# Layer 2: x1 to the output at once, the expert output copied by ScalarE and added there by GpSimd's transfers, for 13 of 16 tiles

## The chip, the core and the metric

The kernel runs on one core of a Trainium2 chip. The core has TensorE (PE in the profile), VectorE (DVE), ScalarE (ACT), GpSimd (POOL) and SyncE (SP), each with its own queue of instructions that it works through in order; they wait for each other through semaphores. Transfers between device memory and the on-chip memory are started by an instruction on an engine's queue and then run on 16 DMA engines beside the five engines. Until now SyncE starts every transfer here. The metric is the time of one execution on the device in microseconds (us).

## The reference: what is computed

The input x has 2048 rows of 576 values. Two layers of two blocks run one after the other with the same weights:

```python
x = A_x
x = x + _A_ref(_layernorm(x), A_wqkv, A_wo)               # linear attention
x = x + _B_ref(_layernorm(x), B_w_q, B_k1, B_k2, B_u, B_v)  # expert layer
x = x + _A_ref(_layernorm(x), A_wqkv, A_wo)
x = x + _B_ref(_layernorm(x), B_w_q, B_k1, B_k2, B_u, B_v)
```

`_A_ref` makes q, k and v (32 heads of 18), passes q and k through phi (t + 1 above 0, exp(t) otherwise), sums k times v over all rows into one state, and gives q times that state over a denominator, times `A_wo`. `_B_ref` scores each row against two small key tables per head, takes the best expert of each head, weighs the chosen rows of `B_v` with gelu of the products with `B_u`, and sums them. The last line's sum is the output: x1, the stream after the second attention, plus the expert output.

## The kernel before

The rows are cut into 16 tiles of 128 rows (t from 0 to 15), so a tile of the stream is 128x576 in float32. A product in float32 is split into a high and a low part on ScalarE and VectorE (`split`, L117 and L118: `hi` by ScalarE's copy, `lo` by VectorE's subtraction) and done in several passes on TensorE. Names in the profile carry a prefix: `thio`/`tloo` are the split attention output of a tile, `thib`/`tlob` the split normalised input of the expert layer (with the expert counts of an earlier tile as a sixth block), `pto`/`ptb` their transposes, `ppo` the product with `A_wo`, `pps` the scores, `ppq` the late q product, `po` the expert output.

In layer 2 a tile passes through these steps, each a generator that stops at its `yield`s, so that the steps of several tiles can be woven together:

- `num` (`back_scale`, L453 to L463): GpSimd makes o from q and the state's sums, VectorE reduces the denominator `den` and divides, GpSimd copies a strip.
- `oT` (`back_oT`): transpose on TensorE, split, a small cast on GpSimd (L468).
- `O` (`back_out`, L483): 28 matrix products into `ppo`; then `residual` (L473), one VectorE instruction that adds x and sums each row, writing x1 (`x11_t`); then the layer norm of x1: GpSimd makes the negative mean `mb` (L187), ScalarE squares and sums (L188, output `junk`), GpSimd makes scale and shift `rsb` (L193 to L195), ScalarE writes the normalised `yb` (L205).
- `bc` (`exp_T`): transposes of `yb` and of the counts `cg` into `ptb`, split.
- `S` (`exp_scores`, L525): 14 products into `pps`, and ScalarE's copy to `s` (L530).
- `sel` (`exp_select`, L553 to L590): thirteen small VectorE instructions that find the experts, ending in `cg`; `gel` (`exp_gelu`, L539 to L545): gelu between ScalarE and GpSimd, in one buffer `g`.
- `po` (`exp_out`, L609): four products into `po`, then the end of the tile. For tiles 0 to 9 and 13 to 15 this is `residual` again: VectorE adds `po` and x1 into x2 (`x21_t`), and SyncE stores it to `out` (L623). For tiles 10, 11 and 12 TensorE has put x1 into `po` beforehand (`base`, L598), and ScalarE copies the finished sum to x2 (L613), which SyncE stores.

The order in which the steps stand on TensorE, ScalarE, VectorE and GpSimd is written out by hand: `play` takes a text such as `O1.4 bc1.3,2x2 sel1.13`, runs one piece of a step for each word (step, layer, tile), and `in_order` holds these four engines to that order. SyncE keeps the order in which its transfers are written. x1 has 6 buffers, x2 has 2, the loaded x has 3, and TensorE's outputs (PSUM) share 4 buffers in turn.

Of the kernel before, what the change touches and what calls it, by code (L numbers as in the profile page):

```python
# [62 lines left out]

@with_exitstack
def network(ctx, tc, x_in, wqkv, wo, wq_t, k_t, u_t, v2, c_mask, c_mask4, c_ident, c_code, c_code1, c_scale, c_shift, out):
    nc = tc.nc
# [117 lines left out]
    def spread(xt, total, n):  # L184

        m = wk.tile([P, 2], F32, tag="mv", name=f"m{n}")
        nc.gpsimd.tensor_scalar(m[:, 0:1], total, -1.0 / D, 1.0, op0=ALU.mult, op1=ALU.mult)  # L187
        nc.scalar.activation(junk, xt, AF.Square, bias=m[:, 0:1], accum_out=m[:, 1:2])  # L188
        return m

    def layernorm_sum(xt, m, n):
        rs = wk.tile([P, 2], F32, tag="rs", name=f"rs{n}")
        nc.gpsimd.tensor_scalar(rs[:, 0:1], m[:, 1:2], 1.0 / D, EPS_LN, op0=ALU.mult, op1=ALU.add)  # L193
# [1 line left out]
        nc.gpsimd.tensor_tensor(rs[:, 1:2], m[:, 0:1], rs[:, 0:1], op=ALU.mult)  # L195
        return normalized(xt, rs, n)

    def normalized(xt, rs, n, vector=False):

        y = wk.tile([P, 2, 320], F32, tag="y", name=f"y{n}", bufs=3)  # L200
        x2 = bass.AP(tensor=xt.tensor, offset=xt.offset, ap=[xt.ap[0], [256, 2], [1, 320]])
        if vector:
            nc.vector.tensor_scalar(y, x2, rs[:, 0:1], rs[:, 1:2], op0=ALU.mult, op1=ALU.add)
        else:
            nc.scalar.activation(y, x2, AF.Identity, scale=rs[:, 0:1], bias=rs[:, 1:2])  # L205
# [270 lines left out]
    def back_out(l, t):  # L476
        n = f"{l}_{t}"
        hl = tt.pop(("oT", l, t))
        p = psum("ppo" + n)
        todo = sorted(out_passes(), key=lambda x: x[1]) if t == 0 else out_passes()  # L480
        for i, (a, b, w, r) in enumerate(todo):
            for c0, c1, at in PARTS:
                nc.tensor.matmul(p[:, at:at + c1 - c0], hl[a][:r, b], w[:r, c0:c1], start=(i == 0), stop=(i == len(todo) - 1))  # L483
# [116 lines left out]
    def exp_out(l, t):  # L600
        n = f"{l}_{t}"
        c = tt.pop(("c", l, t))
        p = tt.pop(("base", l, t), None)
        based = p is not None
        if not based:
            p = psum("po" + n)
        for i in range(2):
            for c0, c1, at in PARTS:
                nc.tensor.matmul(p[:, at:at + c1 - c0], c[i], vmix[:, c0:c1], start=(i == 0 and not based), stop=(i == 1))  # L609
        yield  # L610
        if based:
            x2 = wk.tile([P, D], F32, tag="x2", name=f"x2{n}", bufs=BUFS["x2"])
            nc.scalar.activation(x2, row(p), AF.Copy)  # L613
        else:
            x2, total = residual(p, xs.pop(("b", l, t)), n, "x2")
        if l == 0:
            nc.sync.dma_start(x_d[t], x2)
# [4 lines left out]
        else:
            nc.sync.dma_start(out[t * P:(t + 1) * P, :], x2)  # L623
# [251 lines left out]
    with in_order(*ALL):  # L875

        play("""
            bT0.13 gel0.12 po0.11 sel0.12 v1.10 po0.11x2 gel0.12 num0.15 sel0.12 k1.10 bT0.13 v1.10 sel0.12 fT1.11
            sel0.12 oT0.14 v1.10 fT1.11 O0.14 num0.15 cT0.12 num0.15 k1.10 cT0.12 O0.14 oT0.15 bT0.13 po0.12 S0.13
            O0.14 fT1.11 S0.13 oT0.15 po0.12x3 sel0.13x2 v1.11 gel0.13 fT1.12 gel0.13 oT0.15 O0.14 sel0.13x2 k1.11  # L880
            v1.11 O0.15 fT1.12 O0.15 bT0.14 st1.10 cT0.13 v1.11 bT0.14 S0.14 cT0.13 O0.15 fT1.12 keep1.12 po0.13 k1.11
            S0.14 gel0.14 sel0.14 po0.13 gel0.14 st1.11 po0.13 k1.12 sel0.14x2 po0.13 fT1.13 k1.12 O0.15 v1.12x2
            sel0.14 v1.12 bT0.15 cT0.14x2 st1.12 fT1.13 bT0.15 po0.14 S0.15 po0.14 fT1.13 S0.15 po0.14 ldx1.1 po0.14
            ldx1.3 v1.13 fT1.14 v1.13 sel0.15x3 gel0.15 k1.13 fT1.14 gel0.15 bT0.-1 v1.13 sel0.15 cT0.15 v1.14 cT0.15
            po0.15 k1.13 q1.13 bT0.-1 po0.15 q1.13 v1.14 po0.15x2 v1.14 k1.14 wl1.0 st1.13 fT1.15x2 k1.14 k1.15 v1.15
            rl1.0 st1.14 k1.15 ldq1.13 v1.15x2 rl1.2 st1.15 lq1.0 mk1.0 zs1.0 M1.1 rl1.1 lq1.0 M1.1 rl1.3 ldx1.0 zs1.0
            M1.4x2 M1.3 lq1.1 M1.0 num1.13 num1.0 num1.13 num1.0x2 M1.3 keep1.11 lq1.1 num1.1 M1.0 oT1.0x2 num1.1
            M1.2x2 rl1.4 num1.1 num1.13 lq1.2 O1.0 oT1.1 oT1.13 q1.14 lq1.2 O1.0 oT1.1 O1.0x2 num1.2 q1.14 lq1.3x2
            num1.2 oT1.13 bc1.0,-9 num1.3 O1.1 bc1.0,-9 num1.2 S1.0 O1.1 oT1.2 S1.0 num1.3 lq1.4 gel1.0 num1.3 oT1.2
            O1.1x2 O1.2 bc1.1,-9 sel1.0 gel1.0 ldx1.2 sel1.0 lq1.4 O1.13 rl1.6 bc1.1,-9 sel1.0 num1.4x2 S1.1 O1.2x2  # L890
            ldx1.13 O1.13 S1.1 lq1.6 O1.2 sel1.0 sel1.1 bc1.2,0 rl1.5 ldx1.5 rl1.7 num1.4 oT1.3 ldq1.14 lq1.5 lq1.6
            gel1.1 bc1.2,0 oT1.4 gel1.1 sel1.1 O1.13 rl1.8 sel1.1 S1.2 po1.0 oT1.3 lq1.5 sel1.1 S1.2 O1.3 po1.0 sel1.2
            rl1.9 O1.13 oT1.4 num1.6 bc1.13,1 num1.5 sel1.2 num1.5 lq1.7 bc1.13,1 gel1.2x2 num1.5 S1.13 O1.3 lq1.7
            O1.3x2 num1.6 rl1.11 sel1.2 po1.1 oT1.5 q1.15 oT1.5 ldx1.4 sel1.2 bc1.3,2 po1.1 S1.13 gel1.13 num1.6 O1.4
            bc1.3,2 sel1.13 q1.15 ldx1.6 po1.2 O1.5 oT1.6 ldq1.15 po1.2 sel1.13 num1.14 S1.3 O1.4 lq1.8 O1.4 num1.14
            num1.7 rl1.10 sel1.13 gel1.13 O1.5 num1.14 O1.4 num1.7 S1.3 sel1.13 ldx1.7 sel1.3 oT1.6 num1.7 bc1.4,13
            ldx1.14 bc1.4,13 rl1.12 O1.6 ldx1.8 lq1.8 po1.13 O1.5 gel1.3 O1.5 sel1.3 oT1.7 po1.13 sel1.3 num1.8 O1.6
            S1.4 gel1.3 num1.8 oT1.7 S1.4 sel1.3 sel1.4 gel1.4 sel1.4 oT1.14 bc1.5,3 lq1.9 O1.6 sel1.4 bc1.5,3 S1.5
            po1.3 ldx1.15 O1.6 num1.8 ldx1.11 gel1.4 oT1.8 oT1.14 num1.15 S1.5 sel1.4 bc1.6,4 po1.3 sel1.5 gel1.5
            lq1.9 bc1.6,4 num1.15 O1.14 num1.9 oT1.8 S1.6 O1.14x2 sel1.5 O1.14 S1.6 gel1.5 po1.4 num1.15 sel1.5x2 O1.7  # L900
            po1.4 num1.9 gel1.6 bc1.14,5 O1.7 bc1.14,5 oT1.15 gel1.6 O1.7 sel1.6 num1.9 O1.8 po1.5 S1.14x2 O1.7 po1.5
            oT1.9 sel1.6 O1.8 sel1.6 ldx1.9 O1.8 sel1.6 sel1.14 gel1.14 oT1.15 sel1.14 lq1.10 oT1.9 lq1.10 bc1.7,6x2
            O1.9 gel1.14 O1.8 sel1.14 po1.6 ldx1.10 po1.6 num1.10 S1.7x2 sel1.14 num1.10 O1.9 sel1.7 bc1.8,14 num1.10
            lq1.11 bc1.8,14 po1.14 sel1.7 O1.9 lq1.11 O1.9 gel1.7x2 sel1.7 S1.8 sel1.7 O1.15 S1.8 ldx1.12 gel1.8
            sel1.8 num1.11 po1.14 O1.15 oT1.10 bc1.9,7 gel1.8 sel1.8 bc1.9,7 lq1.12 O1.15 S1.9 sel1.8 oT1.10 num1.11
            sel1.8 lq1.12 O1.15 num1.12 po1.7 S1.9 num1.11 bc1.15,8 gel1.9 po1.7 sel1.9 O1.10 gel1.9 oT1.11 num1.12
            bc1.15,8 O1.10x2 po1.8x2 sel1.9 oT1.11 S1.15x2 sel1.9 O1.11 O1.10 gel1.15 sel1.9 gel1.15 sel1.15 bc1.10,9
            num1.12 O1.11 sel1.15 bc1.10,9 O1.11 oT1.12 S1.10 sel1.15 po1.9 O1.11 sel1.15 oT1.12 S1.10 gel1.10
            bc1.11,15 sel1.10 O1.12 po1.9 gel1.10 bc1.11,15 O1.12x2 S1.11 sel1.10x2 po1.15 sel1.10 po1.15 S1.11
            sel1.11 O1.12 sel1.11 base1.10 bc1.12,10x2 gel1.11x2 sel1.11 S1.12x2 sel1.11 base1.11 gel1.12 sel1.12  # L910
            gel1.12 po1.10 bc1.-1,11x2 base1.12 sel1.12x2 po1.10 sel1.12 po1.11x2 bc1.-1,12x2 po1.12x2
        """)


# [42 lines left out]
```

## Time and profile before

| | |
|---|---|
| time, median of 3 runs | 718.7 us (717.38 to 720.29) |
| the profiled execution's own time | 718.14 us |
| its span, first to last instruction | 716.4 us |
| TensorE busy | 699.6 us, 98% |
| VectorE busy | 475.1 us, 66% |
| ScalarE busy | 321.6 us, 45% |
| GpSimd busy | 201.6 us, 28% |
| mean granted TensorE clock | 0.996 |

The profile is of one execution. A row of its timeline has the start in us from the span's start, the duration in us, the engine, the line, the operation, out<-in with the shapes, how many instructions the row merges, and in brackets how long the engine sat idle before it and whose instruction ended that. Buffer numbers are left out of names, so which tile a row belongs to is found by laying the rows beside the program's own order, which has them. TensorE's instructions are pipelined and their ends are modelled, so that rows of PE overlap a little. The second layer's expert part stands between about 540 us and the end; the first `po` of layer 2 is at 566.7 us.

### The profile page before, as it was taken

The numbers are of one execution on the slowest core, as the hardware profiler recorded it, in microseconds if no ns is written. First come the engines' busy times: TensorE is split into PE (matmuls) and PEld (weight loads), VectorE is DVE, ScalarE is ACT, GpSimd is POOL, SyncE is SP. The second block draws the span as 40 slices with busy tenths as digits, with TensorE's granted clock in tenths as the row PEclk, the third lists the DMA queues.
The fourth block names the chain that finished last, engine by engine and source line by source line (L and its number), as shares of the span: only waits on it lengthen the run. The fifth ranks groups of instructions, "written<-read, shape, count | busy, mean of one in ns | idle before, by whom it ended". The sixth has DMA issues, their size and how long they took to land.

```text
span 716.4 us, 14695 instructions
## 1 busy us (share of the span) xinstructions
PE 699.6 (98%) x5464; PEld 650.7 (91%) x5464; DVE 475.1 (66%) x1031; ACT 321.6 (45%) x658; POOL 201.6 (28%) x543
## 2 busy tenths in 40 slices
PE   9999999999999999999999999999999999999995
PEld 6999989999998999899998999899899999899984
DVE  5533343435437877688787888551647788988996
ACT  5422422343224456455565554644544534454442
POOL 3211000111004533334443433210323234434431
PEclk9999999999999999999999999999999999999998
DMA  9847777765302322566767665514532324111101
GB/s 270 291 164 243 266 234 262 247 192 175 108 1 64 103 101 91 162 216 215 245 218 233 212 196 175 168 44 128 149 120 84 97 86 125 47 67 34 67 17 66
DMA packets 82711, 107.17 MB, mean 150 GB/s; under 512 B 8976, under 2 KB 47376, under 8 KB 82640
## 3 DMA queue, kind: packets, MB, share of 16 engines
q1 hardware_dynamic: 82640, 106.24, 46.5%
q8 instruction: 43, 0.70, 0.4%
q14 instruction: 28, 0.23, 0.1%
HBM read 68.88 MB, written 37.32 MB: 148 GB/s over the span
## 4 chain that ended last, share of the span: by engine, by line
PE 82%; DVE 8%; ACT 4%; issue 2%; DMA 2%; POOL 1%; SPq 0%; DVEq 0%; ACTq 0%; POOLq 0%
PE ppk L258 15%; PE ppv L258 14%; PE ppq L258 14%; PE ppo L483 12%; PE pps L525 7%; PE kva L525 5%; PE kva L360 3%; PE fold_ps L641 2%; PE po L609 2%; PE ptb L215 2%; PE m L414 1%; PE pto L215 1%; DVE x L473 1%; PE ppq L270 1%; PE ppk L270 1%
## 5 line engine op out<-in xcount | busy, mean ns | idle before, releaser
L483 PE MATMUL ppo<-ohi,thio 126*128 126x252 f32 (+1 forms) x320 | 50.5, 300 | 2.6 <-ACT thio L117 2.6
L483 PEld LDWEIGHTS ppo<-ohi,thio 126*128 126x128 f32 (+1 forms) x320 | 44.8, 189 | 4.4 <-ACT thio L117 3.1
L258 PE MATMUL ppk<-whi,thif 128*128 128x252 f32 (+1 forms) x300 | 45.3, 298 | 0.8 <-ACT thif L117 0.8
L188 ACT ACTIVATE junk<-x,mb 128x576 bf16<-128x576 f32 x32 | 24.8, 775 | 45.2 <-POOL mb L187 44.9
L453 POOL TENSOR_TENSOR o<-pq,zb 128x576 f32<-128x576 f32 x19 | 27.4, 1441 | 62.2 <-ACT zb L399 58.6
L258 PE MATMUL ppv<-whi,thif 128*128 128x252 f32 (+1 forms) x300 | 44.7, 295 | 0.1
L258 PEld LDWEIGHTS ppk<-whi,thif 128*128 128x128 f32 x300 | 40.9, 188 | 4.0 <-issue 2.9
L205 ACT ACTIVATE yb<-x,rsb 128x640 f32<-128x640 f32 x32 | 29.5, 921 | 33.3 <-POOL rsb L195 33.3
L179 POOL TENSOR_SCALAR rsf<-mvf 128x1 f32<-128x1 f32 x16 | 3.4, 212 | 145.3 <-DVE mvf L176 145.2
L258 PE MATMUL ppv<-whi,tlof 128*128 128x252 f32 (+1 forms) x300 | 43.9, 293 | 0.0
L258 PE MATMUL ppk<-whi,tlof 128*128 128x252 f32 (+1 forms) x300 | 43.9, 293 | 0.0
L258 PEld LDWEIGHTS ppv<-whi,thif 128*128 128x128 f32 x300 | 41.3, 188 | 1.0 <-issue 0.4
L258 PEld LDWEIGHTS ppk<-whi,tlof 128*128 128x128 f32 x300 | 41.2, 188 | 0.0
L258 PEld LDWEIGHTS ppv<-whi,tlof 128*128 128x128 f32 x300 | 41.2, 188 | 0.0
L483 PE MATMUL ppo<-olo,thio 126*128 126x252 f32 (+1 forms) x256 | 39.6, 293 | 0.0
L258 PE MATMUL ppq<-whi 128*128 128x252 f32 (+1 forms) x260 | 39.5, 299 | 0.0
L483 PE MATMUL ppo<-ohi,tloo 126*128 126x252 f32 (+1 forms) x256 | 39.4, 293 | 0.0
L277 DVE TENSOR_SCALAR ek<-ek 128x576 f32<-128x576 f32 x16 | 7.3, 457 | 46.4 <-ACT ek L276 46.4
L258 PEld LDWEIGHTS ppq<-whi 128*128 128x128 f32 x260 | 36.0, 188 | 0.6 <-DVE eq L287 0.3
L483 PEld LDWEIGHTS ppo<-olo,thio 126*128 126x128 f32 x256 | 36.2, 188 | 0.0
L483 PEld LDWEIGHTS ppo<-ohi,tloo 126*128 126x128 f32 x256 | 36.1, 188 | 0.0
L258 PE MATMUL ppk<-wlo,thif 128*128 128x252 f32 x240 | 36.1, 293 | 0.0
(205 smaller groups left out, 1784.6 us busy)
## 6 DMA issues: line engine op xcount, KB each, us to landing
fold<-in_wq_t SPq DMA_DIRECT2D x64, 288.0 KB
whi<-hl_d SPq DMA_DIRECT2D x26, 320.0 KB
y_df<-rf SPq DMA_DIRECT2D x23, 320.0 KB
...
```

The source lines that it names most:

```text
L188: nc.scalar.activation(junk, xt, AF.Square, bias=m[:, 0:1], accum_out=m[:, 1:2])
L205: nc.scalar.activation(y, x2, AF.Identity, scale=rs[:, 0:1], bias=rs[:, 1:2])
L215: nc.tensor.transpose(pt[:, b * P:(b + 1) * P], x, ident)
L258: nc.tensor.matmul(o[:, at:at + c1 - c0], tt[a == "lo"][:, b, :], wb[:, cols + c0:cols + c1], start=(i == 0), stop=(i == len(todo) - 1))
L270: nc.tensor.matmul(p[:, at:at + c1 - c0], tt[a == "lo"][:, b, :], wb[:, cols + c0:cols + c1], start=(i == 0), stop=(i == len(todo) - 1))
L277: nc.vector.tensor_scalar(e, e, 1.0, EPS, op0=ALU.min, op1=ALU.add)
L360: nc.tensor.matmul(a[64 * h:64 * h + 64, c * 72:c * 72 + n], vt[:, 2 * c + h], fk[:, f0:f0 + n], start=(t == 0 and c == 0), stop=(t == NT ...
L453: nc.gpsimd.tensor_tensor(o[:, :D], pq, zb, op=ALU.mult)
L483: nc.tensor.matmul(p[:, at:at + c1 - c0], hl[a][:r, b], w[:r, c0:c1], start=(i == 0), stop=(i == len(todo) - 1))
L525: nc.tensor.matmul(p[:, :512], hl[a == "lo"][:, b, :], shi[:, b] if w == "hi" else slo[:, blocks(REM)[b][1]], start=(i == 0), stop=(i == l ...
L609: nc.tensor.matmul(p[:, at:at + c1 - c0], c[i], vmix[:, c0:c1], start=(i == 0 and not based), stop=(i == 1))
L641: nc.tensor.matmul(p[32 * j:32 * j + 32, at:at + c1 - c0], kpad[:, ch // 2, 24 - 8 * a:56 - 8 * a], st[:, c0:c1], start=(a == 0), stop=(a ...
```

## The change

For layer 2 and the 13 tiles other than 10, 11 and 12:

- In `O`, after the residual, SyncE stores x1 to `out` at once.
- In `po`, VectorE's `residual` goes. ScalarE copies `po` to x2 (a 128x576 copy out of PSUM), and in a further piece of the step GpSimd starts a transfer that adds x2 to what stands in `out` (`accum_op=ALU.add`).
- The written order gets one more `po` word for each of the 13 tiles, which is where GpSimd's transfer stands. The other words keep their order (the words with `x2` or `x3` are merely written out).

TensorE's instructions and their order stay as they are. The code, with two lines of the table for its look:

```diff
+BASED = (10, 11, 12)
...
         x1, total = residual(p, xs.pop(("a", l, t)), n, "x1")
         xs["b", l, t] = x1
         yield
+        if l == 1 and t not in BASED:
+            xs.pop(("b", l, t))
+            nc.sync.dma_start(out[t * P:(t + 1) * P, :], x1)
         m = spread(x1, total, "b" + n)
...
         yield
-        if based:
+        if l == 1:
             x2 = wk.tile([P, D], F32, tag="x2", name=f"x2{n}", bufs=BUFS["x2"])
             nc.scalar.activation(x2, row(p), AF.Copy)
         else:
...
+        elif based:
+            nc.sync.dma_start(out[t * P:(t + 1) * P, :], x2)
         else:
-            nc.sync.dma_start(out[t * P:(t + 1) * P, :], x2)
+            yield
+            nc.gpsimd.dma_start(out[t * P:(t + 1) * P, :], x2, accum_op=ALU.add)
...
-            rl1.9 O1.13 oT1.4 num1.6 bc1.13,1 num1.5 sel1.2 num1.5 lq1.7 bc1.13,1 gel1.2x2 num1.5 S1.13 O1.3 lq1.7
+            rl1.9 O1.13 oT1.4 po1.0 num1.6 bc1.13,1 num1.5 sel1.2 num1.5 lq1.7 bc1.13,1 gel1.2 gel1.2 num1.5 S1.13 O1.3 lq1.7
```

Three places show how instructions move. In these rows the changed kernel's lines are 3 higher up to the store, and 6 higher behind it (L188 is now L191, L613 is L619); the number behind a name's tile, as 8506 in `mb1_8_8506`, is only a buffer's number.

The first place is around the end of tile 5. ScalarE before, from the square of tile 7 (`junk`, `mb1_7`) to the split of tile 9's attention output:

```order
L188 ACTIVATE junk_85,mb1_7_8404<-x11_7_8388,mb1_7_8404 128x576
L530 ACTIVATE s1_14_8467<-pps1_14_8452 128x512
L205 ACTIVATE yb1_7_8474<-x11_7_8388,rsb1_7_8470 128x640
L188 ACTIVATE junk_85,mb1_8_8506<-x11_8_8495,mb1_8_8506 128x576
L539 ACTIVATE g1_14_8521<-s1_14_8467 128x64
L117 ACTIVATE thio1_15_8399<-pto1_15_8393 128x640
L117 ACTIVATE thio1_9_8486<-pto1_9_8480 128x640
```

and ScalarE now:

```order
L191 ACTIVATE junk_85,mb1_7_8408<-x11_7_8390,mb1_7_8408 128x576
L536 ACTIVATE s1_14_8471<-pps1_14_8456 128x512
L208 ACTIVATE yb1_7_8478<-x11_7_8390,rsb1_7_8474 128x640
L619 ACTIVATE x21_5_8480<-po1_5_8451 128x576
L191 ACTIVATE junk_85,mb1_8_8510<-x11_8_8497,mb1_8_8510 128x576
L545 ACTIVATE g1_14_8525<-s1_14_8471 128x64
```

The copy of tile 5 stands between `yb1_7` and the square of tile 8. GpSimd at the same place, before:

```order
L528 MEMSET s1_14_8467 128x64
L193 TENSOR_SCALAR rsb1_7_8470<-mb1_7_8404 128x1
L194 TENSOR_TENSOR rsb1_7_8470<-rsb1_7_8470,mhalf_72 128x1
L195 TENSOR_TENSOR rsb1_7_8470<-mb1_7_8404,rsb1_7_8470 128x1
L187 TENSOR_SCALAR mb1_8_8506<-sumx11_8_8496 128x1
```

and now:

```order
L196 TENSOR_SCALAR rsb1_7_8474<-mb1_7_8408 128x1
L197 TENSOR_TENSOR rsb1_7_8474<-rsb1_7_8474,mhalf_72 128x1
L198 TENSOR_TENSOR rsb1_7_8474<-mb1_7_8408,rsb1_7_8474 128x1
L632 DMA out<-x21_5_8480 128x576
L190 TENSOR_SCALAR mb1_8_8510<-sumx11_8_8498 128x1
```

Tile 5's transfer, which reads ScalarE's copy, stands ahead of `mb1_8`, which ScalarE's square of tile 8 needs.

The second place is GpSimd where the layer norm of tile 10 is made, before:

```order
L468 CAST tloo1_11_9014<-thio1_11_9013 16x128
L528 MEMSET s1_15_9060 128x64
L193 TENSOR_SCALAR rsb1_10_9098<-mb1_10_9023 128x1
L194 TENSOR_TENSOR rsb1_10_9098<-rsb1_10_9098,mhalf_72 128x1
L195 TENSOR_TENSOR rsb1_10_9098<-mb1_10_9023,rsb1_10_9098 128x1
```

and now:

```order
L471 CAST tloo1_11_9016<-thio1_11_9015 16x128
L534 MEMSET s1_15_9061 128x64
L632 DMA out<-x21_8_9034 128x576
L196 TENSOR_SCALAR rsb1_10_9100<-mb1_10_9026 128x1
L197 TENSOR_TENSOR rsb1_10_9100<-rsb1_10_9100,mhalf_72 128x1
```

Tile 8's transfer stands ahead of the three instructions that make `rsb1_10`.

The third place is ScalarE near the end, where tile 12, the last one, gets its layer norm; before:

```order
L117 ACTIVATE thib1_11_9213<-ptb1_11_9206 128x768
L188 ACTIVATE junk_85,mb1_12_9263<-x11_12_9260,mb1_12_9263 128x576
L530 ACTIVATE s1_11_9281<-pps1_11_9266 128x512
L205 ACTIVATE yb1_12_9322<-x11_12_9260,rsb1_12_9318 128x640
L117 ACTIVATE thib1_12_9341<-ptb1_12_9334 128x768
```

and now:

```order
L191 ACTIVATE junk_85,mb1_12_9263<-x11_12_9260,mb1_12_9263 128x576
L619 ACTIVATE x21_15_9307<-po1_15_9297 128x576
L536 ACTIVATE s1_11_9282<-pps1_11_9267 128x512
L208 ACTIVATE yb1_12_9321<-x11_12_9260,rsb1_12_9317 128x640
L120 ACTIVATE thib1_12_9341<-ptb1_12_9334 128x768
```

The copy of tile 15 stands ahead of `s1_11` and `yb1_12`. On VectorE the 13 instructions of L473 that read `po` are gone, and on SyncE the 13 stores stand behind the x1 of their tile instead of behind its x2.

More of the change, by code (lines that the diff above doesn't have):

```diff
@@ L877, in network @@
         play("""
[L878 to L892, printed above, removed]
@@ L898, in network @@
[L898 to L911, printed above, removed]
+            bT0.13 gel0.12 po0.11 sel0.12 v1.10 po0.11 po0.11 gel0.12 num0.15 sel0.12 k1.10 bT0.13 v1.10 sel0.12 fT1.11
@@ new lines, in network @@
+            O1.11 O1.10 gel1.15 sel1.9 gel1.15 sel1.15 bc1.10,9 num1.12 O1.11 sel1.15 bc1.10,9 O1.11 oT1.12 S1.10
+            sel1.15 po1.9 O1.11 sel1.15 oT1.12 S1.10 gel1.10 bc1.11,15 sel1.10 O1.12 po1.9 gel1.10 bc1.11,15 O1.12 O1.12
+            po1.9 S1.11 sel1.10 sel1.10 po1.15 sel1.10 po1.15 S1.11 sel1.11 O1.12 sel1.11 po1.15 base1.10 bc1.12,10
+            bc1.12,10 gel1.11 gel1.11 sel1.11 S1.12 S1.12 sel1.11 base1.11 gel1.12 sel1.12 gel1.12 po1.10 bc1.-1,11
+            bc1.-1,11 base1.12 sel1.12 sel1.12 po1.10 sel1.12 po1.11 po1.11 bc1.-1,12 bc1.-1,12 po1.12 po1.12
```

34 lines of the change are left out of this document (30 added, 4 removed).

## The prediction

> **What bounds the kernel now.** I read the page's first part, then the busy time by stretches of the stage that changes (columns: stretch, its length, then busy us and instructions of PE, PEld, DVE, ACT and POOL, granted clock, DMA share, GB/s).
>
> ```profile
> PE 699.6 (98%) x5464; PEld 650.7 (91%) x5464; DVE 475.1 (66%) x1031; ACT 321.6 (45%) x658; POOL 201.6 (28%) x543
> 560.00:610.00 50.00, 49.52 (x341) 46.68 (x341) 44.46 (x97) 22.61 (x44) 20.84 (x55) 1.00 0.33 103
> 610.00:690.00 80.00, 79.60 (x531) 74.03 (x529) 72.29 (x175) 38.45 (x75) 33.37 (x94) 1.00 0.14 45
> 690.00:716.40 26.40, 18.40 (x94) 14.70 (x92) 18.80 (x53) 8.31 (x19) 6.01 (x19) 0.89 0.15 57
> ```
>
> VectorE is 90% busy here, and 13 of its instructions go; but TensorE idles only 0.48 us up to 610 and 0.40 us from there to 690. A busy TensorE can hide waits, so I looked whether its blocks stretch; they don't (chain of waits, then TensorE's timeline):
>
> ```profile
> 618.76 3.67 PE ppo L483 x28
> 626.24 3.68 PE ppo L483 x28
> ...
> 609.71 0.33 PE L215 MATMUL ptb<-ident,cg 128*128 128x128 f32 x1 [0.48 <-DVE cg L590]
> 684.98 0.77 PE L215 MATMUL pto<-ident,o 128*128 128x128 f32 x5 [0.40 <-DVE o L461]
> 698.95 0.77 PE L215 MATMUL ptb<-ident,yb 128*128 128x128 f32 x5
> 710.33 0.48 PE L215 MATMUL ptb<-ident,cg 128*128 128x128 f32 x1 [2.75 <-DVE cg L590]
> ```
>
> So TensorE sets the pace to about 698, and VectorE holds it up twice, 0.88 us in all. Behind that comes a serial tail: the last tile's scores, its selection on VectorE, the last `po`, a copy and a store. Relief of VectorE can buy little; what matters is whether the added work on ScalarE and GpSimd, both half idle, makes TensorE wait.
>
> **What each part costs.** The view of the tile `po` (durations are minimum, median, maximum in ns):
>
> ```profile
> L473 DVE SCALAR_TENSOR_TENSOR x<-po,x x29: 718/750/759, 254.2 to 698.2; 128x576 f32<-128x576 f32 x29
> L613 ACT ACTIVATE x<-po x3: 643/651/651, 706.3 to 712.6; 128x576 f32<-128x576 f32 x3
> ```
>
> VectorE loses 13 x 0.75 = 9.8 us. ScalarE gains 13 x 0.65 = 8.5 us, some 0.55 each where instructions follow closely. GpSimd gains 13 starts of a transfer, each of a cost D that no row shows. The bounds are SyncE's start of the same 128x576 store, and GpSimd's whole pass over such a tile:
>
> ```profile
> L623 SPq DMA_DIRECT2D out<-x x16: 332/338/383, 568.2 to 713.3; - x16
> L453 POOL TENSOR_TENSOR o<-eq,zb x13: 1424/1435/1874, 509.8 to 670.5; 128x576 f32<-128x576 f32 x13
> ```
>
> D lies between 0.34 and 1.43 us. A start of a transfer is like the first row, but GpSimd is slow on small things; I take the middle, D = 0.9. The Trainium skill ("DMA: Bandwidth & Descriptors", Specifications) puts the first byte of a GpSimd transfer at about 1 us against 0.6 for SyncE; with D = 1 the sum below would be 0.3 us more. SyncE's stores only move ahead, 0.33 us each. The x loads that stand behind them on SyncE's queue waited for a residual of the same time anyway, to get their buffer, and are read a good tile later: nothing, with that lead as cover; without it, 0.33 us a tile. The additional traffic meets a DMA share of 0.14 to 0.33: nothing. GpSimd's start waits for the store of the same rows, which SyncE issued when x1 was made, a tile or more before: nothing. x2 has two buffers, so a copy waits for the transfer of two tiles earlier; the closest pair, tiles 15 and 11, lies in the tail, where a late copy delays one store: nothing.
>
> Now I set each copy and each start at its place in the order, beside the timeline. Most disappear in gaps. Five places matter; times in brackets are mine.
>
> *Tile 0, before `o` of tiles 6 and 5.* GpSimd's start precedes them, and the denominator waits for them:
>
> ```profile
> 568.22 0.69 ACT L117 ACTIVATE thio<-pto 128x640 fp32r<-128x640 f32 x1
> 569.78 0.82 DVE L118 TENSOR_TENSOR tloo<-pto,thio 128x640 fp32r<-128x640 f32 x1
> 571.16 2.82 POOL L453 TENSOR_TENSOR o<-eq,zb 128x576 f32<-128x576 f32 x2
> 574.02 0.75 DVE L456 TENSOR_REDUCE den<-o 128x32 f32<-128x576 f32 x1
> 582.91 0.29 DVE L590 TENSOR_TENSOR cg<-g,ct 128x128 f32<-128x128 f32 x1
> 583.81 0.27 PE L215 MATMUL ptb<-ident,cg 128*128 128x128 f32 x1
> ```
>
> Tile 0's copy ahead of `thio` lets it end at (569.50), so the relieved VectorE starts `tloo` 0.28 us earlier at most, and GpSimd follows. The chain from 574 to `cg` is then late by D - 0.28. `cg` has 0.55 us to spare (583.20 to 583.81, less a semaphore). Cost D - 0.83: 0.07 us.
>
> *The stall at 609.71.* Here the relief should show, but does it?
>
> ```profile
> 606.68 0.69 ACT L117 ACTIVATE thio<-pto 128x640 fp32r<-128x640 f32 x1
> 607.99 0.81 DVE L118 TENSOR_TENSOR tloo<-pto,thio 128x640 fp32r<-128x640 f32 x1
> 607.78 0.32 POOL L545 TENSOR_TENSOR g<-g,s 128x64 f32<-128x64 f32 x1
> ```
>
> Tile 13's copy goes just ahead of this `thio`, which then ends at (607.95): VectorE's `tloo` can't start before the 607.99 it had, and `cg`, four instructions on, stays at 609.37. Tile 13's start stands two instructions ahead of L545, which `cg` reads, and pushes its end from 608.10 to about 608.06 + D = (608.96), still in time. The stall stays: gain 0.
>
> *Tile 5: GpSimd waits for ScalarE, and ScalarE then for GpSimd.*
>
> ```profile
> 637.16 0.21 POOL L195 TENSOR_TENSOR rsb<-mb,rsb 128x1 f32<-128x1 f32 x1
> 638.09 0.19 POOL L187 TENSOR_SCALAR mb<-sumx 128x1 f32<-128x1 f32 x1 [0.71 <-DVE x L473]
> 638.62 0.60 ACT L530 ACTIVATE s<-pps 128x512 f32<-128x512 f32 x1 [3.97 <-PE pps L525]
> 639.11 0.91 ACT L205 ACTIVATE yb<-x,rsb 128x640 f32<-128x640 f32 x1
> 639.92 0.76 ACT L188 ACTIVATE junk<-x,mb 128x576 bf16<-128x576 f32 x1
> 640.68 0.24 ACT L539 ACTIVATE g<-s 128x64 f32<-128x64 f32 x1
> 640.83 1.28 ACT L117 ACTIVATE thio<-pto 128x640 fp32r<-128x640 f32 x2
> 643.23 1.58 PE L483 MATMUL ppo<-ohi,thio 126*128 126x252 f32 x10
> ```
>
> The copy runs behind `yb`, (639.93 to 640.58). GpSimd, done with `rsb` at 637.4, sits before its start until then. Behind it stands `mb` of tile 8, which went at 638.09 and now ends at (640.65 + D + 0.25). ScalarE's square (`junk`) waits for it, starting at (640.95 + D) instead of 639.92; then come `g` and two `thio`, 2.20 us to the second one's end, plus a semaphore: (643.2 + D). TensorE wants it, tile 9's, at 643.23. Cost D - 0.05: 0.85 us, once and for all, since TensorE is full before and behind.
>
> *Tile 8: `rsb` of tile 10.* GpSimd's start goes between the memset and `rsb`:
>
> ```profile
> 680.17 0.15 POOL L528 MEMSET s<- 128x64 f32 x1
> 680.29 0.19 POOL L193 TENSOR_SCALAR rsb<-mb 128x1 f32<-128x1 f32 x1
> 681.45 0.93 ACT L205 ACTIVATE yb<-x,rsb 128x640 f32<-128x640 f32 x1 [0.56 <-POOL rsb L195]
> 684.99 0.23 POOL L463 COPY o<-o 128x56 f32<-128x56 f32 x1 [0.68 <-DVE o L461]
> ```
>
> `yb` and the gelu behind it are late by D + 0.1, and with them GpSimd's L463, which waited 0.68 us for VectorE and so loses D - 0.55. The last transposes of 684.98 read that strip. Cost D - 0.55, at least 0.15 (tile 8's copy also pushes a `thio` in VectorE's way at 678.9): 0.35 us.
>
> *Tile 15: the last `yb`.* Before, VectorE emptied `po`; now ScalarE does, ahead of `s` and `yb`:
>
> ```profile
> 697.56 0.43 PE L609 MATMUL po<-vmix,tlob 128*128 128x252 f32 x2
> 697.49 0.60 ACT L530 ACTIVATE s<-pps 128x512 f32<-128x512 f32 x1 [1.21 <-PE pps L525]
> 697.98 0.91 ACT L205 ACTIVATE yb<-x,rsb 128x640 f32<-128x640 f32 x1
> ```
>
> `po` of tile 15 ends at 697.99. The copy runs from (698.03), `s` from (698.58), `yb` from (699.05) instead of 697.98. The transposes at 698.95 wait for `yb`, and everything behind is the serial tail. Cost 1.07 us, whatever D is; tile 9's start, between `mb` and `rsb` of tile 12, hides behind this up to D = 2.
>
> The sum: 0.07 + 0 + 0.85 + 0.35 + 1.07 = 2.3 us, so 718.14 becomes 720.5 for the profiled execution; that one lies 0.56 us below the runs' median, and on the median it is **721.0 us**. At D = 0.34: 0 + 0.29 + 0.15 + 1.07 = 1.5 (720.2). At D = 1.43: 0.60 + 0.17 + 1.38 + 0.88 + 1.07 = 4.1 (722.8).
>
> **Rivals.** (a) *GpSimd's start is longer than its tile pass.* GpSimd and VectorE do hold each other up: VectorE's L569 of 128x32 takes 1.34 us at 571.29 beside GpSimd's `o`, and 0.19 elsewhere.
>
> ```profile
> 571.29 1.34 DVE L569 SCALAR_TENSOR_TENSOR cd<-m 128x32 bf16<-128x32 bf16 x1
> ```
>
> If a start is blocked in the same way for one VectorE instruction of up to 0.95 us (`tlob`), D reaches 2.4: 1.57 + 1.14 + 2.35 + 1.85 and 1.4 in the tail are 8.3 us, 727.0. The Trainium skill ("SBUF — State Buffer", the "DVE blocks DMA" trap) states just this for VectorE's fast copies, 3.1 us against 0.62; few VectorE instructions here are of such a kind. It decides from D = 1.3, where the loss passes 0.5%. (b) *VectorE is the true bound*, and TensorE's modelled ends hide the waits: then about half of the 9.8 us comes back, 714. Against it stand the even `ppo` blocks. (c) *The pushes are absorbed*: GpSimd's spans are rough, D is near zero, or ScalarE has more room than I read; the two stalls go and the tail stays, 718.7 - 0.9 + 1.1 = 718.9. For it speaks that both engines are half idle; against it, that the tail's `yb` has no slack.
>
> **How the numbers follow.** Measured kernels here can't be told apart below 0.5%, 3.6 us: faster is below 715.1, slower above 722.3. My forecast gets 0.50, (a) 0.28, (b) 0.04, (c) 0.18. Slower takes (a) and the forecast's upper edge, 0.31; faster is (b), 0.04; the same 0.65. The range runs from (c) with some scatter, 717.5, to near (a), 726.
>
> **What would show it.** Right: GpSimd's L632 near 0.9 us; a wait of TensorE for `thio` near 643 and for `yb` near 699, both where the rows above show none; the 0.48 us stall still there; VectorE idler by some 10 us. Wrong: no wait near 643 (D small or the order shields it), or L632 beyond 1.4 us, or `ppo` blocks that get shorter, which would be (b).

## The result, and the profile after

The changed kernel takes 725.15 us (median; 723.21 to 726.67) beside 719.07 us for the kernel before on the same chip (717.38 to 720.29): 6.1 us more, a ratio of 1.008 with an interval of 1.0064 to 1.0096. The prediction had 721.0 us and a range of 717.5 to 726, and the range holds the time. But its likeliest verdict was "the same", and by the boundary that it set (slower above 722.3 us) the kernel is slower, which had a chance of 0.31.

The first part of the page of the changed kernel, and its busy time by stretches (columns as in the prediction):

```profile
PE 701.9 (97%) x5464; PEld 651.6 (90%) x5464; DVE 466.6 (64%) x1005; ACT 329.1 (45%) x671; POOL 214.0 (30%) x556
```

```profile
560.00:610.00 50.00, 49.83 (x345) 47.00 (x344) 38.06 (x83) 25.12 (x48) 22.91 (x55) 1.00 0.46 118
610.00:690.00 80.00, 77.72 (x516) 71.51 (x515) 67.31 (x154) 40.08 (x79) 39.88 (x99) 1.00 0.37 75
```

The work moved about as forecast: VectorE 8.5 us less (forecast 9.8), ScalarE 7.5 and GpSimd 12.4 us more (8.5 and 11.7). But TensorE, with the same instructions in the same order, now idles 2.3 us of the 80 behind 610 where it idled 0.4. Its waits, in the timeline of the changed kernel:

```profile
586.22 0.33 PE L218 MATMUL ptb<-ident,cg 128*128 128x128 f32 x1 [0.17 <-DVE cg L596]
612.55 0.33 PE L218 MATMUL ptb<-ident,cg 128*128 128x128 f32 x1 [0.84 <-DVE cg L596]
647.58 1.56 PE L486 MATMUL ppo<-ohi,thio 126*128 126x252 f32 x10 [0.83 <-DVE tloo L121]
676.13 0.77 PE L218 MATMUL ptb<-ident,yb 128*128 128x128 f32 x5 [0.18 <-ACT yb L208]
689.88 0.66 PE L218 MATMUL pto<-ident,o 128*128 128x128 f32 x4 [0.21 <-DVE o L464]
691.37 0.33 PE L218 MATMUL pto<-ident,o 128*128 128x128 f32 x1 [0.84 <-POOL o L466]
705.69 0.77 PE L218 MATMUL ptb<-ident,yb 128*128 128x128 f32 x5 [1.07 <-ACT yb L208]
707.52 1.96 PE L531 MATMUL pps<-shi,thib 128*128 128x512 f32 x5 [0.96 <-ACT thib L120]
```

Before, two of these stood there (0.48 for cg, 0.40 for o) besides the last one, which was 0.96 then too. The one at 647.58, a product with thio (tile 5's place), and the one for yb of the last tile (tile 15's) are those the prediction named; but what ends the first is VectorE's `tloo`, not thio. GpSimd's starts of the 13 transfers, in the view of the tile `out`:

```profile
L632 POOL DMA_DIRECT2D out<-x x13: 870/939/1088, 573.0 to 704.6; - x13
...
  ACT x L619: 6.9, 4
  issue: 1.1, 5
...
DMA to landing us min/median/max: 4.1/4.3/7.6
```

A start takes 0.94 us, against the 0.9 that the prediction took for D.

**Where the time went, place by place.** TensorE works through the same list in both kernels, so the start of a product in its timeline can be compared with its start in the profile before (tile 9's first product with thio: 643.23 before, 647.58 now, 4.35 later), and the growth of that shift over a stretch is what the stretch lost. The first row gives the shift of each profile on entering the changed section, 571 us in the profile before. All of it is there at 520 us, ahead of the first early store of x1 (525.8 us in the changed kernel), so it is scatter between executions. e1 to e10 are the experiments below; e5, the changed kernel profiled again, is within 0.06 us of the column "changed" at every place.

| us lost at | forecast | changed | e1 | e2 | e3 | e4 | e6 | e7 | e8 | e9 | e10 |
|---|---|---|---|---|---|---|---|---|---|---|---|
| (before the section) | | 1.90 | 1.25 | 0.18 | -0.01 | -0.23 | -0.49 | -0.18 | -0.22 | 0.33 | 1.57 |
| tile 0, 571 to 592 | 0.07 | 0.55 | 0.54 | 0 | 0 | 0.54 | 0.54 | 1.45 | 0 | 0.27 | 0 |
| 592 to 600 | 0 | 0.02 | 0.04 | 0 | 0 | 0.46 | 0.01 | 0.91 | 0 | 0 | 0.01 |
| tile 13, to 630 | 0 | 0.37 | 0.35 | -0.20 | -0.19 | 0.77 | 0.35 | 1.11 | -0.21 | 0.12 | -0.20 |
| PSUM for tile 10's ppq, to 639 | 0 | 0.41 | 0.39 | 0.39 | 0.42 | 0.11 | 0.03 | 0.42 | -0.01 | 0.39 | 0.04 |
| tile 5, to 659 | 0.85 | 1.08 | 1.08 | 0 | 0.01 | 0.01 | 0.01 | 1.96 | 0.02 | 0.76 | 0.01 |
| tile 14, to 677 | 0 | 0.45 | 0.43 | 0.47 | 0.05 | 0.05 | 0.40 | 1.27 | 0.05 | 0.12 | 0.05 |
| tile 8, to 694 | 0.35 | 0.89 | 0.89 | 0.45 | 0.30 | -0.07 | 0.86 | 1.76 | -0.30 | 0.84 | -0.30 |
| tile 15, to 699 | 1.07 | 1.07 | -0.01 | -0.01 | 1.07 | 0 | 1.07 | 1.06 | -0.01 | 1.06 | 1.07 |
| lower clock, to 704 | 0 | 1.53 | 0.01 | 0 | 0.01 | 0 | 1.47 | 0.02 | 0.01 | 1.47 | 0.01 |
| sum of the section | 2.3 | 6.37 | 3.72 | 1.10 | 1.67 | 1.87 | 4.74 | 9.96 | -0.45 | 5.03 | 0.69 |
| median over before | 2.3 | 6.1 | 4.5 | 1.3 | 2.3 | 2.0 | 3.6 | 10.0 | -0.6 | 5.1 | 1.8 |

So the waits lose 4.8 us in the changed kernel, and the clock 1.5 more in this profile, whose own execution took 726.67 us. The last row is against the kernel before as it ran beside each: 717.95 us for e1 to e4, 718.48 for e6 to e8, 718.18 for e9 and e10.

### The profile page after: what moved, and what is told of

The parts are those of the page before. It is cut to its first block, busy times and chain, and to the rows that moved or that the text cites. A ratio compares the mean times of both kernels' runs of the same rounds, so it can differ in the third digit from the quotient of the medians.

```text
span 724.9 us, 14693 instructions
## 1 busy us (share of the span) xinstructions
PE 701.9 (97%) x5464; PEld 651.6 (90%) x5464; DVE 466.6 (64%) x1005; ACT 329.1 (45%) x671; POOL 214.0 (30%) x556
## 4 chain that ended last, share of the span: by engine, by line
PE 78%; DVE 7%; ACT 6%; POOL 3%; issue 3%; DMA 2%; SPq 0%; ACTq 0%; DVEq 0%; POOLq 0%
PE ppk L261 13%; PE ppv L261 13%; PE ppq L261 13%; PE ppo L486 12%; PE pps L531 8%; PE kva L531 4%; PE kva L363 3%; PE fold_ps L650 2%; PE po L615 2%; PE ptb L218 2%; DMA go<-y_do 2%; PE m L417 1%; PE pto L218 1%; PE ppk L273 1%; PE ppq L273 1%
## 5 line engine op out<-in xcount | busy, mean ns | idle before, releaser
L191 ACT ACTIVATE junk<-x,mb 128x576 bf16<-128x576 f32 x32 | 24.9, 778 | 45.9 <-POOL mb L190 45.8
L261 PE MATMUL ppv<-wlo,thif 128*128 128x252 f32 x240 | 36.1, 293 | 0.0
```

What stands on the lines that cost most here:

```text
L261: nc.tensor.matmul(o[:, at:at + c1 - c0], tt[a == "lo"][:, b, :], wb[:, cols + c0:cols + c1], start=(i == 0), stop=(i == len(todo) - 1))
```

## The experiments

Theory: what costs is where the new instructions stand. A start of GpSimd (0.94 us) and a copy of ScalarE (0.65) wait in queues ahead of a mean, a gelu or a normalised tile that TensorE wants soon. Rivals: the transfers themselves (traffic, accumulation, landing); the copies alone; the starts alone; VectorE as the true bound. Diffs are against the changed kernel unless said; a word of the order's text is one piece of a step.

**e1: tile 15's copy behind the last yb.**

```diff
-sel1.10 sel1.10 po1.15 sel1.10 po1.15 S1.11 sel1.11 O1.12 sel1.11 po1.15
+sel1.10 sel1.10 po1.15 sel1.10 S1.11 sel1.11 O1.12 po1.15 sel1.11 po1.15
```

> The changed kernel (6.1 us over the kernel before) with one move: tile 15's copy on ScalarE stands behind s of tile 11 and yb of tile 12 instead of ahead of them. Theory (a copy ahead of the last yb is pure delay, and the two idle gaps that it opens on TensorE bring the granted clock down for the last scores): 1.1 us come back by the delay alone and 1.5 more if the clock stays at 1.00 over the 14 products of tile 12's scores, so 3.5 to 5.0 us over the kernel before. Rival (the transfers and their traffic cost, the place of a copy does not): unchanged, 6 us over.

722.48 us, ratio 1.0065 (1.0052 to 1.0078), 4.5 us over. The wait for yb is gone (-0.01 in the table), and in this profile the clock stays at 1.00 until tile 12's scores are done. Tile 15's 1.07 us is the copy's place.

**e2: the starts of tiles 0, 13, 5, 14 and 8 moved as well.**

```diff
-O1.13 oT1.4 po1.0 num1.6
+O1.13 oT1.4 num1.6
-O1.3 O1.3 num1.6 rl1.11
+O1.3 O1.3 num1.6 po1.0 rl1.11
-S1.4 po1.13 gel1.3
+S1.4 gel1.3
-ldx1.15 O1.6 num1.8
+ldx1.15 O1.6 po1.13 num1.8
-sel1.6 po1.5 ldx1.9 O1.8 sel1.6
+sel1.6 ldx1.9 O1.8 po1.5 sel1.6
-gel1.8 po1.14 sel1.8
+gel1.8 sel1.8
-lq1.12 O1.15 num1.12 po1.7
+lq1.12 O1.15 po1.14 num1.12 po1.7
-S1.15 S1.15 po1.8 sel1.9 O1.11 O1.10 gel1.15
+S1.15 S1.15 sel1.9 O1.11 O1.10 po1.8 gel1.15
```

> The same work as the changed kernel, but six of its pieces stand elsewhere: tile 15's copy as in e1, and GpSimd's starts of tiles 0, 13, 5, 14 and 8 each behind the mean, the last step of the normalization or the gelu that it stood ahead of. Theory (order on GpSimd and ScalarE makes the loss): the waits of TensorE for cg near 612, thio near 647, yb near 676 and 706 and o near 691 go back to what they were before, and the kernel is 0.5 to 2 us over the kernel before; what is left is the longer hold of a PSUM buffer by po. Rival (transfers and traffic): 4 to 6 us over. Rival (VectorE was the true bound and its relief had only been hidden): below the kernel before by 2 us or more.

719.29 us, ratio 1.0018 (1.0008 to 1.0028), 1.3 us over: of 6.1 us, 4.8 come back by order alone. Three places are left: the PSUM wait (0.39), tile 8's copy, still ahead of a thio (0.45 with tile 8's start), and a new loss of my own making: I put tile 14's start directly ahead of GpSimd's `o` of tile 12, and VectorE's division of another tile, which runs beside both, got longer. VectorE's row in e2, and the same one before:

```profile
671.09 2.90 DVE L464 TENSOR_TENSOR o<-eq,r 128x576 f32<-128x576 f32 x1
```

```profile
670.68 1.83 DVE L461 TENSOR_TENSOR o<-eq,r 128x576 f32<-128x576 f32 x1
```

**e3: copies, but no starts on GpSimd.**

```diff
-            nc.gpsimd.dma_start(out[t * P:(t + 1) * P, :], x2, accum_op=ALU.add)
+            nc.sync.dma_start(out[t * P:(t + 1) * P, :], x2)
```

> The changed kernel with GpSimd's 13 accumulating transfers replaced by plain stores from SyncE at the same place of the program. It leaves out the addition of x1 to the expert output for 13 tiles; ScalarE's 13 copies, the early stores of x1 and the order of everything else stay. Theory (starts on GpSimd and copies on ScalarE each cost at their places): the costs of tiles 0, 13, 5, 14 and 8 vanish and those of the copies stay: 1.1 us at tile 15, 0.4 where ppq of tile 10 waits for a PSUM buffer, and up to 1.5 by the clock of the tail: 1.5 to 3 us over the kernel before. Rival (the accumulation in the transfers costs): 0 to 0.5 over. Rival (the copies alone make the loss): 5 to 6 over.

720.23 us, ratio 1.0029 (1.0018 to 1.004), 2.3 us over. The copies cost exactly at tile 15 (1.07), the PSUM wait (0.42) and tile 8 (0.30), and tile 13's place even gains 0.19: the relief of VectorE, visible once no start stands ahead of the gelu.

**e4: starts, but no copies.** The kernel before, with its 13 stores issued by GpSimd at the changed kernel's places.

```diff
-            nc.sync.dma_start(out[t * P:(t + 1) * P, :], x2)
+            yield
+            nc.gpsimd.dma_start(out[t * P:(t + 1) * P, :], x2)
```

> The kernel before with one change: the 13 stores of x2 are started by GpSimd (plain, not accumulating) at the places where the changed kernel has its accumulating transfers. VectorE adds x1 as before, x1 is not stored early, ScalarE copies nothing. Theory (0.94 us of GpSimd's queue at each place, and tile 5 costs only because the start waits for a copy that ScalarE makes behind yb): tile 0 0.4 (no relief of VectorE), tile 13 up to 0.4, tile 8 0.4, tile 14 up to 0.4, tile 5 and tile 15 nothing: 0.8 to 1.6 us over the kernel before. Rival (starts alone make the loss): 4 to 6 over. Rival (only the copies or the accumulation cost): 0 to 0.3 over.

719.94 us, ratio 1.003 (1.002 to 1.0039), 2.0 us over, a little above the forecast: the place of tile 13 and the stretch ahead of it cost 1.23 us, where VectorE still has its 13 additions. Tiles 5, 14 and 8 cost nothing; that was forecast for tile 5, but up to 0.4 us for each of the others. So e3 and e4 together (1.67 + 1.87 in their profiles) make 3.5 of the 4.8 us. At tile 5 the loss needs both, a start that waits for a copy (e6). The other places of GpSimd's starts can't be read from e4 alone, because the start of a plain transfer is also 0.3 us shorter, and lands earlier:

```profile
L629 POOL DMA_DIRECT2D out<-x x13: 582/642/788, 571.1 to 700.9; - x13
...
DMA to landing us min/median/max: 2.4/2.5/4.0
```

**e5: the changed kernel again.** No edit.

> The changed kernel once more, nothing edited, to see which of its losses are in every execution. Theory: the waits of TensorE for cg, thio, o and yb at the named places come again to within 0.1 us, 4.8 us together with the PSUM wait; the 1.5 us of lower granted clock over tile 12's scores need not come again, nor the 1.9 us that its first profile had gained ahead of the changed section. 4.5 to 6.5 us over the kernel before. Rival (the lower clock in the tail follows from the two idle gaps of 1 us): it is there again.

723.69 us, ratio 1.0077 (1.0061 to 1.0094), 5.2 us over. Every place repeats, and so does the lower clock in the tail (1.48 us). The shift ahead of the section was 0.82 instead of 1.90: that part of the first profile was scatter.

**e6: tile 5's copy where ScalarE idles.**

```diff
-O1.8 po1.5 S1.14 S1.14 O1.7 po1.5 oT1.9
+O1.8 po1.5 S1.14 po1.5 S1.14 O1.7 oT1.9
```

> The changed kernel with one move: tile 5's copy on ScalarE stands ahead of s of tile 14 (where ScalarE idles for 4 us) instead of behind s and yb. GpSimd's start then has its data before it is its turn. Theory (tile 5 costs because the start waits for the copy, and mb of tile 8 behind it): the wait for thio near 647 goes, 1.1 us, and with it perhaps the 0.4 us in which ppq of tile 10 waits for a PSUM buffer: 1.1 to 1.5 us below the changed kernel, 3.3 to 5 over the kernel before. Rival (the 0.94 us start alone delays mb): 0 to 0.2 below the changed kernel.

722.05 us, ratio 1.0057 (1.0041 to 1.0074): 3.6 us over, 1.6 below e5. Both the wait at tile 5 (1.08 to 0.01) and the PSUM wait (0.41 to 0.03) are gone. In the changed kernel's timeline the chain stands row by row:

```profile
642.80 0.64 ACT L619 ACTIVATE x<-po 128x576 f32<-128x576 f32 x1
643.73 0.94 POOL L632 DMA_DIRECT2D out<-x  x1 [4.01 <-ACT x L619]
644.75 0.18 POOL L190 TENSOR_SCALAR mb<-sumx 128x1 f32<-128x1 f32 x1
644.97 0.78 ACT L191 ACTIVATE junk<-x,mb 128x576 bf16<-128x576 f32 x1 [1.53 <-POOL mb L190]
645.89 1.27 ACT L120 ACTIVATE thio<-pto 128x640 fp32r<-128x640 f32 x2
```

GpSimd sits 4.01 us before its start, for a copy that ScalarE makes late, and everything behind follows. In e6 the copy is done in time, and the same start delays nobody:

```profile
635.78 0.65 ACT L619 ACTIVATE x<-po 128x576 f32<-128x576 f32 x1 [0.88 <-PE po L615]
637.58 0.94 POOL L632 DMA_DIRECT2D out<-x  x1 [0.30 <-issue]
638.59 0.18 POOL L190 TENSOR_SCALAR mb<-sumx 128x1 f32<-128x1 f32 x1
```

**e7: twice the starts, the same bytes.**

```diff
-            nc.gpsimd.dma_start(out[t * P:(t + 1) * P, :], x2, accum_op=ALU.add)
+            for c in (0, D // 2):
+                nc.gpsimd.dma_start(out[t * P:(t + 1) * P, c:c + D // 2], x2[:, c:c + D // 2], accum_op=ALU.add)
```

> The changed kernel with each of GpSimd's 13 accumulating transfers issued as two, of 288 columns each; all else stays. It doubles the number of starts (26 of some 0.9 us) and not the bytes. Theory (a start's time on GpSimd's queue is paid once at each place that has no slack): 0.9 us more at each of tiles 0, 13, 5, 14 and 8, and in the tail what tile 9's start no longer hides (up to 0.5): 4 to 5 us above the changed kernel, 9 to 11 over the kernel before. Rival (the landing of the transfers or their traffic costs): 0 to 1 above the changed kernel. Rival (a start's time goes by its bytes): L632 falls to some 0.5 each, 0 to 0.5 above.

728.48 us, ratio 1.015 (1.0129 to 1.017), 10.0 us over. The places of tiles 0, 13, 5, 14 and 8 cost 0.7 to 0.9 us more each, and 592 to 600 another 0.9. A start's time doesn't go by its bytes. The view mixes the first and the second start of a pair: the first, of half the bytes, took 0.94 us (median), as the whole one did, and the second 1.19, of which 0.28 run beside the first. Each half still has 128 rows, so whether the time goes by rows is not shown.

```profile
L633 POOL DMA_DIRECT2D out<-x x26: 871/1122/1213, 570.9 to 708.3; - x26
```

**e8: the same work at better places.** As e2, but tile 5 as in e6 and two further words:

```diff
-lq1.12 O1.15 S1.9 sel1.8 oT1.10
+lq1.12 O1.15 po1.14 S1.9 sel1.8 oT1.10
-po1.8 po1.8 sel1.9 oT1.11 S1.15 S1.15 po1.8 sel1.9 O1.11 O1.10 gel1.15
+po1.8 sel1.9 oT1.11 po1.8 S1.15 S1.15 sel1.9 O1.11 O1.10 po1.8 gel1.15
```

> The same work as the changed kernel, with the places of e2 improved by its profile: tile 5's copy ahead of s of tile 14 (as in e6) and its start where the changed kernel has it, tile 8's copy behind thio of tile 11 instead of ahead, tile 14's start directly behind mb of tile 15 (GpSimd idles there for 2 to 3 us); tiles 0, 13 and 15 as in e2. Theory: nothing of the loss is left, and the relief of VectorE shows at cg near 609 (0.2 us, as in e2): 0.5 us below to 0.3 above the kernel before, no measurable difference. Rival (something in the change costs wherever it stands): 1 us or more over. Rival (VectorE's 9.8 us were a bound): 2 us or more below.

717.87 us, ratio 0.9996 (0.9987 to 1.0005): no difference from the kernel before that can be told. Every wait of TensorE in its section and tail:

```profile
609.29 0.33 PE L218 MATMUL ptb<-ident,cg 128*128 128x128 f32 x1 [0.28 <-DVE cg L596]
700.10 1.43 PE L531 MATMUL pps<-shi,thib 128*128 128x512 f32 x5 [0.96 <-ACT thib L120]
709.65 0.33 PE L218 MATMUL ptb<-ident,cg 128*128 128x128 f32 x1 [2.75 <-DVE cg L596]
710.35 0.85 PE L615 MATMUL po<-vmix,thib 128*128 128x252 f32 x2 [0.37 <-ACT thib L120]
```

All 13 copies, starts, early stores and accumulations are there, so nothing in the change costs by itself that these runs can tell (the interval ends 0.4 us above the kernel before), and the section is 0.45 us shorter than before: the stall for cg is 0.28 instead of 0.48, the one for o gone. That is all that 9.8 us of relief for VectorE bring in this order.

**e9: plain transfers instead of accumulating ones.**

```diff
-            nc.gpsimd.dma_start(out[t * P:(t + 1) * P, :], x2, accum_op=ALU.add)
+            nc.gpsimd.dma_start(out[t * P:(t + 1) * P, :], x2)
```

> The changed kernel with GpSimd's 13 transfers plain instead of accumulating; place, queue and size stay. It leaves out the addition of x1 to the expert output for 13 tiles. In e4 a plain start took 0.64 us where the accumulating one takes 0.94, and landed after 2.5 us instead of 4.3. Theory (a start's time on the queue is paid at tiles 0, 13, 5, 14 and 8): 0.3 us less at each of these, up to 1.5 in all, while the PSUM wait (0.4), tile 15's copy (1.1) and the clock of the tail stay: 3.3 to 5 us over the kernel before. Rival (the accumulation's longer landing or its reads of the output cost): 2 us or more below the changed kernel, under 3 over. Rival (the start's length doesn't matter): as the changed kernel, 5 to 6 over.

723.26 us, ratio 1.0066 (1.0053 to 1.008), 5.1 us over: just above the theory's 3.3 to 5 and inside the last rival's 5 to 6, so the places must tell. Its starts take 0.64 us, and four places pay 0.25 to 0.33 us less than in the changed kernel (tiles 0, 13, 5, 14: 0.27, 0.12, 0.76, 0.12). That they fall by what the start is shorter (0.30) speaks for its length; the landing, 1.8 us sooner, shows at no other place. Tile 8 doesn't fall (0.84), and the rows tell why. Behind tile 8's start, GpSimd's product of the gelu comes to stand beside VectorE's division in both kernels, and in both it ends 0.18 us behind it, so that an earlier start of it gains nothing. In the changed kernel and, behind it, in e9:

```profile
689.02 0.80 DVE L464 TENSOR_TENSOR o<-eq,r 128x576 f32<-128x576 f32 x1
689.30 0.70 POOL L547 TENSOR_TENSOR g<-g,s 128x64 f32<-128x64 f32 x1
```

```profile
686.23 0.76 DVE L464 TENSOR_TENSOR o<-eq,r 128x576 f32<-128x576 f32 x1
686.26 0.91 POOL L547 TENSOR_TENSOR g<-g,s 128x64 f32<-128x64 f32 x1
```

Without a start ahead of it (e3) the same product took 0.32 us.

**e10: e8 with tile 15's copy ahead of the last yb again.** The diff of e1, backwards.

> e8 with one place put back as in the changed kernel: tile 15's copy ahead of s of tile 11 and yb of tile 12. Theory (this copy costs by itself, whatever the rest does): 1.07 us over e8 by the wait for yb, so 0.4 over the kernel before where the granted clock stays at 1.00 over tile 12's scores, and 1.5 us more in the executions in which it falls, which goes by where the two gaps of 1 us fall: median 0.3 to 2 us over the kernel before. Rival (the clock falls in each such execution): 1.7 to 2.1 over. Rival (it costs only together with the other losses): as e8, 0.6 below.

720.01 us, ratio 1.0026 (1.0014 to 1.0039), 1.8 us over the kernel before, where e8 was 0.3 below it by its ratio. The wait is 1.07 us again, alone. The median would fit the rival that has the clock fall each time, but the profile excludes it: the same two gaps stand there, and the clock stays at 1.00. The other 1.0 us between the two ratios would fit executions in which it falls; how many did is not shown.

## The clock in the tail

Where tile 15's copy stands ahead of the last yb, TensorE idles 1.07 us and, 0.9 us later, 0.96 us more; the second gap stands in the profile before too. In the changed kernel the granted clock (the third number from the end) then drops to half, and comes back 3.4 us later:

```profile
704.76:708.18 3.41, 1.53 (x9) 1.21 (x10) 3.04 (x9) 1.82 (x4) 1.15 (x3) 1.00 0.67 92
708.18:711.59 3.41, 3.41 (x10) 2.64 (x9) 2.50 (x7) 0.26 (x1) 0.94 (x4) 0.50 0.01 1
711.59:715.00 3.41, 3.41 (x19) 2.83 (x17) 1.57 (x5) 1.57 (x5) 0.94 (x3) 1.00 0.00 0
```

In e10 the same gaps were followed by full clock:

```profile
698.18:701.59 3.41, 2.35 (x14) 1.70 (x14) 2.14 (x8) 1.95 (x3) 1.56 (x3) 1.00 0.62 86
701.59:705.00 3.41, 2.45 (x13) 1.86 (x12) 3.24 (x9) 1.21 (x3) 1.24 (x5) 1.00 0.62 86
705.00:708.42 3.41, 3.41 (x18) 2.89 (x17) 2.25 (x8) 0.99 (x3) 0.66 (x3) 1.00 0.00 0
```

Of the seven profiles with both gaps it fell in four (changed, e5, e6, e9: 1.47 to 1.53 us each) and not in three (e3, e7, e10); of the five without the first gap it fell in none ahead of the end of tile 12's scores.

The traces show what goes with it. In all twelve, the clock changes only a whole number of windows of 3.413 us after it first rose: in the changed kernel it rises at 5.03 us and falls 206 windows later, at 708.18. The stretches above are cut at these windows. In the four profiles that fell, both gaps lie in one window, which has 1.87 to 1.94 us idle; in the three others a window ends between the gaps (in e10 at 701.59), and neither has more than 1.07. It holds beyond the tail: of the 2488 full windows at full clock in the twelve traces, 16 were followed by half clock, each with 1.83 us idle or more, and all others have 1.80 or less. Where the windows lie was left to chance and set by no run, and TensorE's ends are modelled, so the boundary near 1.8 us is what these traces show and no more.

The Trainium skill ("TensorE: Matmul & The Clock Gate", Part 1) has the clock set by a free-running window of about 3.4 us, so that it depends on the run where a gap falls in it. The windows here agree with that. The table of the Trainium skill there asks for an idle window; here one that was 45% busy was enough.

In how many executions the clock falls I can't say from the profiles alone; the medians of the changed kernel and of e5 (6.1 and 5.2 us over, 4.8 without the clock) fit with some but not all.

## Why the prediction was right, and where not

- **What bounds the kernel**: right. TensorE sets the pace, and relief of VectorE buys little: e8 has all of it and gains 0.45 us in its profile. Rival (b) falls. So does rival (c), that the pushes are absorbed: they show as waits.
- **D = 0.9**: right, 0.94 measured; as the middle of two bounds 1.1 us apart, in part by luck. Rival (a), D of 1.3 or more because VectorE blocks the starts, falls: the longest of the 13 took 1.09 us. The time came near its lower end for other reasons.
- **What a start takes from the queue**: the step that failed, a mis-sized term. I counted D; at the places that cost, the queue loses another 0.2 to 0.4 us around it (at tiles 1, 3 and 4 GpSimd goes to the start without a gap). At tile 0, GpSimd goes from the cast's end at 572.75 to `o` at 574.12, 1.37 us, of which the start is 1.09:

```profile
572.40 0.35 POOL L471 CAST tloo<-thio 16x128 fp32r<-16x128 f32 x1 [3.91 <-DVE tloo L121]
572.96 1.09 POOL L632 DMA_DIRECT2D out<-x  x1 [0.21 <-issue]
574.12 2.82 POOL L456 TENSOR_TENSOR o<-eq,zb 128x576 f32<-128x576 f32 x2
```

  With 1.37 in place of D, "D - 0.83" gives 0.54, and 0.55 was measured. At tile 5, it is 1.49 us from the copy's end (643.44) to the end of mb (644.93), where D + 0.32 had 1.26.
- **Tile 5, 0.85**: right place, 1.08 lost, and the last link is another. The copy ended 0.4 us earlier than forecast (640.19 in the times of the profile before, by the shift of 3.25 us up to there), so in spite of the longer start tile 9's thio ended no later than forecast: at 647.16, which stands for 643.91, where "643.2 + D" gives 644.1. TensorE starts only at 647.58, behind VectorE's `tloo` of tile 15, whose PSUM buffer tile 9's `ppo` takes over; and that `tloo` can start only behind the first of the two delayed thio. The row now, and the same one before, when it was done 0.65 us ahead of the product at 643.23:

```profile
646.61 0.82 DVE L121 TENSOR_TENSOR tloo<-pto,thio 128x640 fp32r<-128x640 f32 x1 [2.69 <-ACT thio L120]
```

```profile
641.76 0.82 DVE L118 TENSOR_TENSOR tloo<-pto,thio 128x640 fp32r<-128x640 f32 x1
```

- **The stall for cg (tile 13), "gain 0"**: wrong on both sides. The relief is worth 0.2 us (e2, e3, e8). And "608.06 + D" for the end of the gelu came out too low:

```profile
609.90 0.16 POOL L534 MEMSET s<- 128x64 f32 x1
610.38 0.95 POOL L632 DMA_DIRECT2D out<-x  x1 [0.32 <-ACT g L549]
611.41 0.23 POOL L550 TENSOR_SCALAR g<-g 128x64 f32<-128x64 f32 x1
611.73 0.32 POOL L551 TENSOR_TENSOR g<-g,s 128x64 f32<-128x64 f32 x1
```

  The shift here is 2.47 us (the first three rows of the table), so the gelu's end at 612.05 stands for 609.58 in the times of the profile before: 0.62 behind the forecast's 608.96. The two instructions behind the start were in the formula. Most of the difference is that GpSimd sits 0.32 us before the start, and that the memset ahead of it ends 0.22 us later than before (607.59 for 607.37). That used up the slack, and the stall grew from 0.48 to 0.84.
- **"Most disappear in gaps"**: wrong for tile 14. Its start stands ahead of mb of tile 15, on which hang ScalarE's square, a thio, GpSimd's cast and only then rsb and yb: 0.45 us, the same pattern that I had worked out for tile 5 and didn't look for elsewhere. e8 puts that start directly behind mb, and 0.05 is left.
- **A cost that I had no term for**: the copy empties `po` of tile 5 later than VectorE did (642.80 here, 635.57 before), and tile 10's ppq gets another of the four PSUM buffers. The order with its waits shows it for the first product of tile 10's ppq, before and now:

```
L258 MATMUL ppq1_10_8535<-whi_76 128x252 [waits DMAHW7_49,DVE_49]
L261 MATMUL ppq1_10_8539<-whi_76 128x252 [waits DMAHW3_49,Activation_49]
```

  It waits for ScalarE's `s` of tile 14 in place of VectorE, as the weight load's row says: 0.41 us, gone in e6 where the copy comes earlier.

```profile
641.48 0.60 ACT L536 ACTIVATE s<-pps 128x512 f32<-128x512 f32 x1 [4.14 <-PE pps L531]
...
642.13 1.35 PEld L261 LDWEIGHTS ppq<-whi 128*128 128x128 f32 x10 [0.38 <-ACT s L536]
```

- **Tile 8, 0.35**: right place, too small; 0.89. Of it 0.30 is the copy ahead of thio (e3), which the prediction put at 0.15 or more, and the rest needs the start. The forecast had neither the 0.34 us that GpSimd sits before this start nor that the gelu's product, so late, takes 0.70 us beside VectorE's division (e9).
- **Tile 15, 1.07**: within 0.01 us in all seven profiles that have it. That the gaps could cost clock was not in the prediction; it is worth 1.5 us in four of the seven.
- **SyncE's stores, the loads behind them, the traffic, at nothing**: no place in the profiles shows them, and e8 contains them all without loss.

With D = 0.94 the prediction's formulas give 2.46 us. The misses add 0.44 (tile 0), 0.37 (13), 0.41 (PSUM), 0.19 (5), 0.45 (14) and 0.50 (8): 4.8 us, the sum of the waits. That the range holds the time is in part luck: its upper end came from rival (a), which fell, and what lies above 721.0 us is these misses and, in some executions, the clock.
